# Filler matmuls in an attention kernel: one more use of TensorE wherever it has had little to do

## The chip, the cores and the metric

One core of one Trainium2 chip. The metric is the device time of one execution in microseconds (us), the median over several; lower is better. A run's profile gives a span that is about 1.7 us shorter than its device time (1177.7 against 1179.46 us for the profile of the kernel before).

## The reference, cut to what matters

Two attention blocks over 2048 tokens, width 1024, 32 heads of 32, in bf16; their outputs stand side by side.

```python
# A: full attention
qkv = (x @ wqkv) ...;  p = softmax(q k^T * 32**-0.5);  o = p v;  out_A = o @ wo
# B: four segments of 512 tokens, causal inside a segment, with a memory M, z carried between them
p = softmax(q k^T * 32**-0.5 + mask);  a_dot = p v
a_mem = (phi(q) M) / (phi(q) z + 1e-6)          # phi(t) = t+1 if t>0 else exp(t)
o = g * a_mem + (1 - g) * a_dot;  M += phi(k)^T v;  z += sum phi(k);  out_B = o @ wo
out = concatenate([out_A, out_B], -1)
```

In both blocks every score needs one exponential, which ScalarE computes. TensorE computes the projections, the scores and the sums (probabilities times V, and probabilities times ones for the denominators).

## The kernel before

The program is written by a planner that runs on the host. It keeps a clock for each engine with an estimated cost for every operation, and at each step it gives TensorE one of three things: scores (as soon as ScalarE has freed their banks), sums, or a piece of a "side" task such as a projection. If there is nothing to do, it lets TensorE's planned clock run on by 0.05 us and looks again. Each engine is then given its list in this order, with semaphores wherever the planner found a dependency. Planned times decide the order only.

```python
def op(self, eng, fn, r=(), w=(), cost=0.1, mode="F"):
    if eng == "PE":
        if mode != self.mode:
            cost += DRAIN                      # the planner's cost (0.105) of a change between scores, sums and full matmuls
        self.mode = mode
    op = Op(eng, self.n[eng], fn); ...
    t = self.free[eng]
    for d in op.deps:
        t = max(t, d.end + LAT)
    op.end = t + cost
    self.free[eng] = op.end
# ... (cut)
# the end of the planner's loop, reached when nothing could be given to TensorE
            if now < WARM and gap >= 0.15:     # WARM = 60: only in the first 60 us
                spare = [...]                  # a free bank
                if spare:
                    R.op("PE", lambda e, bank=spare[0]: e.matmul(self.ps[:, bank, :], self.ones[:, :], ...128x512 of ones...,
                                                                 start=True, stop=True), r=["ones"], w=[("ps", spare[0])], cost=MM)
                    gap = 0.0
                    continue
            R.free["PE"] = now + 0.05
            gap += 0.05
```

So fillers existed already, but only in the first 60 planned microseconds. A projection is a sum of eight matmuls into one bank and may be cut into parts, between which other work runs. The sums of the attention gather in one bank (`OLB`) over the 16 key tiles of a unit. A bank in which such a sum is under way must not be overwritten. (A second program for inputs that would overflow the exponential stands in the file too; it did not run here.)

Of the kernel before, what the change touches and what calls it, by code (L numbers as in the profile page):

```python
# [11 lines left out]
P = 128  # L12
# [9 lines left out]
MM = 0.213  # L22
# [14 lines left out]
class Recorder:  # L37
# [5 lines left out]
    def __init__(self, nc, es, tag):  # L43
        self.nc = nc
        self.tag = tag
        self.all = []
        self.n = {e: 0 for e in self.ENG}
        self.free = {e: 0.0 for e in self.ENG}
        self.last = {e: None for e in self.ENG}
        self.lastw, self.readers = {}, {}  # L50
        self.sem = {e: es.enter_context(nc.semaphore(f"{tag}_{e.lower()}")) for e in self.ENG if e != "SP"}
        self.ch_sem = [es.enter_context(nc.semaphore(f"{tag}_dma{i}")) for i in range(self.NCH)]
        self.ch_last = [None] * self.NCH
        self.ch_n = [0] * self.NCH
        self.ch_next = 0
        self.mode = None
        self.pipe = 0.0

    def _deps(self, eng, r, w):
        deps = []  # L60
# [18 lines left out]
            self.readers[k] = {}  # L79

    def op(self, eng, fn, r=(), w=(), cost=0.1, mode="F"):
        if eng == "PE":
            if mode != self.mode:
                cost += DRAIN
            self.mode = mode
        op = Op(eng, self.n[eng], fn)
        self.n[eng] += 1
        op.deps = self._deps(eng, r, w)
        self._note(op, r, w)
        t = self.free[eng]  # L90
        for d in op.deps:
            t = max(t, d.end + LAT)
        op.end = t + cost
        self.free[eng] = op.end
        self.all.append(op)
        self.last[eng] = op
        return op

    def dma(self, fn, r=(), w=(), issue=0.1, mb=0.25, q="SP", turn=False):
        c = self.ch_next  # L100
        self.ch_next = (c + 1) % self.NCH
        op = Op(f"D{c}", self.ch_n[c], fn)
        self.ch_n[c] += 1
        op.deps = self._deps(op.eng, r, w)
        if self.ch_last[c] is not None:
            op.deps.append(self.ch_last[c])
        self.ch_last[c] = op
        op.dma, op.queue = c, q
        self._note(op, r, w)
        t = self.free[q]  # L110
        for d in op.deps:
            t = max(t, d.end + LAT)
        self.free[q] = t + issue
        if turn:

            op.end = t + issue + 2.2
        else:
            self.pipe = max(self.pipe, t + issue) + mb / 0.22
            op.end = self.pipe + 1.5
        self.all.append(op)  # L120
        return op

    def resolve(self):
        names = list(self.ENG) + [f"D{i}" for i in range(self.NCH)]
# [109 lines left out]
SLOPE = 0.65  # L234
STICK = True
WARM = 60
TILES = (0, 1, 2, 3)
ON_ACT = ()
AHEAD = (6, 7)
# [8 lines left out]
class Kernel:  # L248
# [215 lines left out]
    def constants(self):  # L464
        R = self.R

        def pool(f, w, r=()):
            R.op("POOL", f, r=r, w=w, cost=0.3)
        R.op("DVE", lambda e: e.memset(self.PT[:, RING - 1, :], 1.0), w=[("PT", RING - 1)], cost=0.2)
        nb = sum(len(b) for b in SLOTS)  # L470
        for b in range(nb):
            R.op("DVE", lambda e, b=b: e.memset(self.ps[:, b, :], 0.0), w=[("ps", b)], cost=0.4)

        R.op("ACT", lambda e: e.activation(self.gcol[:, 0, :], self.PT[:, RING - 1, 0:8], ACTF.Exp), r=[("PT", RING - 1)], w=["gcol"], cost=1.5)
        pool(lambda e: e.memset(self.blk32[:, :], 1.0), ["blk32"])
        pool(lambda e: e.affine_select(self.blk32[:, :], self.blk32[:, :], pattern=[[-32, 4], [0, 8]],
                                       compare_op=ALU.is_ge, fill=0.0, base=0, channel_multiplier=1), ["blk32"])
        pool(lambda e: e.affine_select(self.blk32[:, :], self.blk32[:, :], pattern=[[32, 4], [0, 8]],
                                       compare_op=ALU.is_ge, fill=0.0, base=31, channel_multiplier=-1), ["blk32"])
        pool(lambda e: e.memset(self.ones[:, :], 1.0), ["ones"])  # L480
        pool(lambda e: e.memset(self.ident[:, :], 0.0), ["ident"])
        pool(lambda e: e.affine_select(self.ident[:, :], self.ident[:, :], pattern=[[-1, P]],
                                       compare_op=ALU.not_equal, fill=1.0, base=0, channel_multiplier=1), ["ident"])
        for i in range(2):
            pool(lambda e, i=i: e.memset(self.VB[i][:, :, :], 1.0), [("VB", i)])
        pool(lambda e: e.memset(self.maskbd[:, :], 1.0), ["maskbd"])
        pool(lambda e: e.affine_select(self.maskbd[:, :], self.maskbd[:, :], pattern=[[-32, 4], [0, 32]],
                                       compare_op=ALU.is_ge, fill=0.0, base=0, channel_multiplier=1), ["maskbd"])
        pool(lambda e: e.affine_select(self.maskbd[:, :], self.maskbd[:, :], pattern=[[32, 4], [0, 32]],
                                       compare_op=ALU.is_ge, fill=0.0, base=31, channel_multiplier=-1), ["maskbd"])  # L490
        pool(lambda e: e.memset(self.Mf[:, :, :], 0.0), [("Mf", g) for g in range(NG)])
# [226 lines left out]
    def mm_run(self, mms, r, w, each, k0=1):  # L718

        R = self.R  # L720
        i = 0
        while i < len(mms):
            room = yield ("pe", self.ready(r(i, i + k0)))
            k = max(k0, min(len(mms) - i, int((room - DRAIN) / each)))
            if len(mms) - i - k < k0:
                k = len(mms) - i
            part = mms[i:i + k]

            def f(e, part=part):
                for o, l, rh, a, z in part:  # L730
                    ins = e.matmul(o, l, rh, start=a, stop=z)  # L731
                return ins
            R.op("PE", f, r=r(i, i + k), w=w, cost=each * k)
            i += k

    def proj_T(self, W, wkey, xsl, xkeys, dst, dkeys, n=512):

# [297 lines left out]
        self.events.add(("out" + kind, c))  # L1035


    def spawn(self, gen, prio, name):
        t = Task(gen, prio if isinstance(prio, tuple) else (prio, 0), name)
        if t.req is not None:  # L1040
            self.tasks.append(t)
            self.tasks.sort(key=lambda t: t.prio)
# [69 lines left out]
    def schedule(self):  # L1112
# [2 lines left out]
        self.qA = [Item([Unit("A", NQ * g + c, g, c, 0, g % 2)]) for g in range(NG) for c in range(NQ)]  # L1115
        self.qB = [Item([Unit("B", 8 * s + g, g, s, half, g % 2) for half in (1, 0)]) for s in range(4) for g in range(NG)]
        self.pvq, self.nseq, self.ol_end, self.run = [], 0, 0.0, None
        self.tasks = []
        self.posA, self.ring, self.ring_busy, self.out_free = 0, 0, set(), [0, 1]
        self.slot_end = {s: 0.0 for s in SLOTS}  # L1120
        self.ring_len = LONG
# [11 lines left out]
        while True:  # L1133
# [52 lines left out]
            for what in (first, "side" if first == "pv" else "pv"):  # L1186
                if done:
                    break
                if what == "pv" and self.pvq:
                    u, st, part = self.pvq[0]  # L1190
                    c = DRAIN + 2 * u.steps[st][part][2] * 0.000417
                    t = u.steps[st][part][0]
                    v = ("vA", u.g, t // 4) if u.kind == "A" else ("vB", u.kn)
                    vk = ("VA", u.buf, t // 4) if u.kind == "A" else ("VB", u.buf)
                    if v in ev and self.ready([vk]) <= now and all((st, h) in u.pend for h in range(4)) \
                            and max(u.pend[(st, h)] for h in range(4)) + 0.15 <= now \
                            and (st > 0 or part > 0 or self.ol_end <= now) \
                            and (st < len(u.steps) - 1 or u.seq < 2 or ("fin", u.seq - 2) in ev) \
                            and (c <= room or len(self.ring_busy) > self.ring_len - 4):
                        if OLB not in self.bank_busy:  # L1200
                            self.emit_pv(u, st, part)
                            self.pvq.pop(0)
                            done = True
                elif what == "side":
                    if full and self.pvq and self.slots:

                        u, st, _ = self.pvq[0]
                        vt = self.ready([("VA", u.buf, u.steps[st][0][0] // 4)]) if u.kind == "A" else 0.0
                        if now < vt < now + 1.5:
                            room = min(room, max(0.5, vt - now))  # L1210
                    for t in self.tasks:
                        if t.req[0] == "pe" and self.satisfied(t.req, now) and room > 0.3:
                            self.resume(t, room)
                            done = True
                            break
# [4 lines left out]
                continue  # L1220
            if cur is None and not self.qA and not self.qB and not self.pvq and not self.tasks:
                break
            if now < WARM and gap >= 0.15:

                spare = [b for b in self.banks if b not in self.bank_busy and self.bank_end[b] <= now]
# [59 lines left out]
```

## Time and profile before

| | before |
|---|---|
| median of 4 runs | 1178.74 us (1176.4 to 1178.82) |
| ScalarE (ACT) busy | 1123.4 us, 95% |
| TensorE (PE) busy | 1069.7 us, 91% |
| mean granted TensorE clock | 0.972 |
| stretches at half clock between 60 and 1150 us | 8, together 54.6 us |

From the page of the kernel before: the busy times of the engines, the row of the granted clock (40 equal slices of the span, in tenths of full speed), the shares of the chain that ended last, and the largest group of instructions.

```profile
span 1177.7 us, 37192 instructions
PE 1069.7 (91%) x16874; PEld 480.1 (41%) x16874; DVE 795.6 (68%) x1368; ACT 1123.4 (95%) x1254; POOL 114.3 (10%) x192
...
PEclk9999999999999998989999998989999998999998
...
ACT 49%; PE 43%; DVE 6%; issue 1%; DMA 1%; DVEq 0%
...
L584 ACT ACTIVATE PT<-ps 128x1024 bf16<-128x1024 f32 (+1 forms) x1184 | 1074.0, 1043 | 31.7 <-PE ps L544 30.1
```

ScalarE is the engine to feed: 1184 exponentials, and most of its idle time (30.1 us) ended when scores arrived from TensorE. The clock row has five slices below 9 ahead of the tail, all in the middle. A slice is 29 us, so the row shows that the clock was cut but not how.

The table of windows shows how. The columns are the window, its length, then busy time and number of instructions of each engine, the granted clock, and the DMA share and rate. Kernel before:

```profile
core 0: us, PE busy (x) PEld busy (x) DVE busy (x) ACT busy (x) POOL busy (x), PEclk, DMA share, GB/s
447.35:450.77 3.42, 1.39 (x40) 0.69 (x40) 3.32 (x4) 3.42 (x6) 1.41 (x3) 1.00 0.00 0
450.77:461.01 10.24, 8.66 (x111) 3.48 (x104) 7.94 (x13) 9.04 (x11) 3.83 (x6) 0.50 0.01 2
519.03:522.45 3.42, 1.53 (x44) 0.57 (x32) 3.02 (x5) 3.42 (x5) 0.27 (x1) 1.00 0.00 0
522.45:532.69 10.24, 8.31 (x106) 3.38 (x103) 7.90 (x14) 9.30 (x11) 3.48 (x6) 0.50 0.01 2
```

In the 3.42 us before a stretch, TensorE is 41% or 45% busy while ScalarE is fully busy: TensorE waits for ScalarE (its longest pauses there are 1.27 and 1.23 us), and no other work stands in its list there. Then the clock goes to one half for 10.24 us, and now ScalarE is idle for 1.2 and 0.9 us of it: scores that came in time at full clock come too late.

### The profile page before, as it was taken

To read this page: it belongs to the slowest core of one execution; us is meant where nothing else is said; L and a number is where in the kernel's file an instruction comes from. 1 tells how busy PE (TensorE), PEld (TensorE's weight loads), DVE (VectorE), ACT (ScalarE), POOL (GpSimd) and SP (SyncE) were. 2 spreads that over 40 slices of the span, in tenths; PEclk is the share of its full clock that TensorE was granted. 3 is DMA by queue.
4 is the path that set the end of the run, shared out by engine and by line. 5 is a ranking of instruction groups with operands and counts; after the bars stand their busy time and mean duration, and the time that the engine had idled before them with its cause. 6 is when DMAs were issued, how large, how long until landed. Compare 5 with 4: busy or idle time off the path is not lost.

```text
span 1177.7 us, 37192 instructions
## 1 busy us (share of the span) xinstructions
PE 1069.7 (91%) x16874; PEld 480.1 (41%) x16874; DVE 795.6 (68%) x1368; ACT 1123.4 (95%) x1254; POOL 114.3 (10%) x192
## 2 busy tenths in 40 slices
PE   7999999999999987989999988889998998799995
PEld 3444444443444433434344433334443443344442
DVE  3366667678686787677768768777677786864444
ACT  5999999999999999999999998989999999999993
POOL 1010012011111011011110111111012011200000
PEclk9999999999999998989999998989999998999998
DMA  7544143152121230401311221111230121200111
GB/s 170 108 90 102 38 100 60 34 108 65 42 46 34 60 73 11 91 20 32 88 30 41 55 60 38 38 33 33 47 80 27 33 47 35 81 19 29 38 38 66
DMA packets 207050, 65.93 MB, mean 56 GB/s; under 512 B 200227, under 2 KB 200227, under 8 KB 206883
## 3 DMA queue, kind: packets, MB, share of 16 engines
q1 hardware_dynamic: 204512, 62.41, 23.6%
q8 instruction: 134, 2.20, 0.8%
q10 hardware_dynamic: 2370, 1.05, 0.4%
q14 instruction: 34, 0.27, 0.1%
HBM read 36.70 MB, written 8.39 MB: 38 GB/s over the span
## 4 chain that ended last, share of the span: by engine, by line
ACT 49%; PE 43%; DVE 6%; issue 1%; DMA 1%; DVEq 0%
ACT PT L584 47%; PE ps L731 23%; PE ps L633 11%; PE ps L544 8%; DVE SQ L656 2%; DVE OL L643 1%; ACT E L921 1%; DVE OL L691 0%; ACT WoB L584 0%; DMA OTA<-in_A_x_dram 0%; DVE outsb L1025 0%; DVE KQB L741 0%; DVE OL L682 0%; DVE KA L741 0%; DVE OTA L660 0%
## 5 line engine op out<-in xcount | busy, mean ns | idle before, releaser
L584 ACT ACTIVATE PT<-ps 128x1024 bf16<-128x1024 f32 (+1 forms) x1184 | 1074.0, 1043 | 31.7 <-PE ps L544 30.1
L633 PE MATMUL ps<-PT,ones 128*32 128x256 bf16 (+1 forms) x4736 | 285.7, 274 | 0.0
L633 PE MATMUL ps<-PT,VA 128*32 128x256 bf16 x3968 | 244.4, 278 | 17.5 <-ACT PT L584 9.9
L656 DVE RECIPROCAL SQ<-OL 128x128 f32<-128x128 f32 x256 | 242.4, 948 | 4.4
L544 PE MATMUL ps<-QA,KA 32*128 32x256 bf16 x4096 | 207.1, 277 | 35.0 <-ACT PT L584 26.5
L731 PE MATMUL ps<-xA,WA 128*128 128x512 bf16 (+1 forms) x792 | 200.7, 387 | 4.0 <-DVE amem L955 1.0
L731 PE MATMUL ps<-xB,WB 128*128 128x512 bf16 x768 | 195.0, 382 | 7.2 <-DVE den L941 3.6
L604 POOL TENSOR_SCALAR_AFFINE_SELECT PT<-PT 128x512 bf16<-128x512 bf16 x128 | 84.1, 659 | 788.5 <-ACT PT L584 783.0
L633 PEld LDWEIGHTS ps<-PT,VA 128*32 128x32 bf16 x3968 | 105.4, 96 | 108.0 <-issue 65.1
L544 PEld LDWEIGHTS ps<-QA,KA 32*128 32x128 bf16 x4096 | 61.3, 93 | 214.3 <-ACT PT L584 186.2
L633 PEld LDWEIGHTS ps<-PT,ones 128*32 128x32 bf16 x4736 | 128.0, 98 | 2.5
L643 DVE COPY OL<-ps 128x512 f32<-128x512 f32 x128 | 85.5, 668 | 32.5 <-PE ps L633 30.9
L731 PEld LDWEIGHTS ps<-xA,WA 128*128 128x128 bf16 x792 | 66.8, 100 | 94.8 <-issue 33.4
L731 PEld LDWEIGHTS ps<-xB,WB 128*128 128x128 bf16 x768 | 62.1, 97 | 94.0 <-issue 41.9
L948 DVE RECIPROCAL den<-den 128x128 f32<-128x128 f32 x96 | 91.0, 948 | 2.0
L1028 DVE CAST outsb<-ps 128x512 bf16<-128x512 f32 x56 | 38.3, 683 | 73.6 <-PE ps L731 71.4
L741 DVE CAST KQB<-ps 128x512 bf16<-128x512 f32 x64 | 43.6, 681 | 52.5 <-PE ps L731 52.4
L731 PE MATMUL ps<-WoB,OTB 128*128 128x512 bf16 x256 | 64.6, 382 | 2.0 <-DVE OTB L684 0.8
L731 PE MATMUL ps<-xA,OTA 128*128 128x512 bf16 x256 | 65.8, 388 | 0.1
L691 DVE SCALAR_TENSOR_TENSOR OL<-OL,SQ 128x256 f32<-128x256 f32 x128 | 58.9, 460 | 4.4
L633 PE MATMUL ps<-PT,VB 128*32 128x256 bf16 (+1 forms) x768 | 48.6, 271 | 10.8 <-DVE OL L643 8.6
L741 DVE CAST VT<-ps 128x512 bf16<-128x512 f32 x32 | 21.9, 685 | 44.7 <-PE ps L731 44.7
(78 smaller groups left out, 540.5 us busy)
## 6 DMA issues: line engine op xcount, KB each, us to landing
WB<-in_B_wk_dram SPq DMA_DIRECT2D x32, 256.0 KB, 3.0
WB<-in_B_wq_dram SPq DMA_DIRECT2D x32, 256.0 KB, 3.0
WB<-in_B_wv_dram SPq DMA_DIRECT2D x32, 256.0 KB, 3.3
out_dram<-outsb SPq DMA_DIRECT2D x32, 256.0 KB, 2.1
WA<-in_A_wqkv_dram SPq DMA_DIRECT2D x22, 256.0 KB, 3.6
WoB<-in_B_wo_dram SPq DMA_DIRECT2D x8, 256.0 KB, 3.4
xA<-in_A_wo_dram SPq DMA_DIRECT2D x8, 256.0 KB, 3.7
OTA<-in_A_x_dram ACTq DMA_DIRECT2D x2, 256.0 KB, 5.0
```

The lines of the kernel that those rows point to most:

```text
L544: ins = e.matmul(o, l, r, start=True, stop=True)
L584: op = R.op("ACT", lambda e: e.activation(self.pt(s0, n)[:, :, 0:width], self.ps[:, banks[0]:banks[0] + n, 0:width], ACTF.Exp, bias=cb, sc ...
L604: mo = R.op("POOL", lambda e, ap=ap, pat=pat: e.affine_select(ap, ap, pattern=pat, compare_op=ALU.is_ge, fill=0.0, base=0, channel_multipl ...
L633: ins = e.matmul(o, l, r, start=start, stop=end, skip_group_check=True)
L643: R.op("DVE", lambda e: e.tensor_copy(self.OL[x][:, :], self.ps[:, OLB, :]), r=[("ps", OLB)], w=[("OL", x)], cost=0.66)
L656: R.op("DVE", lambda e, cs=cs: e.reciprocal(rec[:, cs], L[:, cs]), r=[ko], w=[k], cost=0.93)
L691: R.op("DVE", lambda e: e.scalar_tensor_tensor(L, L, 1.0, rec, ALU.mult, ALU.add, accum_out=self.rng[:, u.seq:u.seq + 1]), r=[k, ko], w=[k ...
L731: ins = e.matmul(o, l, rh, start=a, stop=z)
L741: op = self.R.op("DVE", lambda e: e.tensor_copy(dst, self.ps[:, bank, 0:n]), r=[("ps", bank)], w=dkeys, cost=0.12 + n * 0.00105)
L921: ex = R.op("ACT", lambda e: e.activation(self.E[:, k0:k1, :], KQ[:, k0:k1, :], ACTF.Exp), r=[("KQB", b, k) for k in range(k0, k1)], w=["E ...
L948: R.op("DVE", lambda e, cs=cs: e.reciprocal(self.den[:, cs], self.den[:, cs]), r=["den"], w=["den"], cost=0.9)
L1028: op = R.op("DVE", lambda e, ns=ns, bank=bank, ob=ob: e.tensor_copy(self.outsb[ob][:, ns], self.ps[:, bank, :]), r=[("ps", bank)], w=[("ou ...
```

## The change

Its intent: keep TensorE's recent activity above a floor, so that the clock is not cut. When the planner finds nothing to do after 60 us, 0.1 us has passed so, and the planned work of the last 3 us is below 66%, it adds one 128x512 matmul. If a sum is under way, the filler has zero weights and is added onto that sum, which it is not to alter. If no sum is open, it overwrites a free bank with ones times ones. (`diag[0]` is a tile that this program does not use otherwise; it is set to zero at the start.)

```diff
+        if eng == "PE":
+            self.spans.append((op.end - bare, op.end))     # bare: the cost without DRAIN
+    def worked(self, now, span):
+        total = 0.0
+        for a, z in reversed(self.spans):
+            if z <= now - span:
+                break
+            total += z - max(a, now - span)
+        return total / span
+KEEP = 0.66
+    def keep_up(self):
+        R = self.R
+        onto = [("ps", OLB)] * self.ol_open + list(self.sums)
+        if not onto:
+            now = R.free["PE"]
+            for b in self.banks:
+                if b not in self.bank_busy and self.bank_end[b] + 0.3 <= now:
+                    R.op("PE", lambda e, b=b: e.matmul(self.ps[:, b, :], self.ones[:, :], ...ones, 512 columns...,
+                                                       start=True, stop=True), r=["ones"], w=[("ps", b)], cost=MM)
+                    return True
+            return False
+        bank = onto[0][1]
+        R.op("PE", lambda e: e.matmul(self.ps[:, bank, :], self.diag[0][:, :], ...ones, 512 columns...,
+                                      start=False, stop=False, skip_group_check=True), r=["zeros", "ones"], w=onto[:1], cost=MM)
+        return True
             if cur is None and not self.qA and not self.qB and not self.pvq and not self.tasks:
                 break
+            if not self.shifted and now >= WARM and gap >= 0.1 and R.worked(now, 3.0) < KEEP and self.keep_up():
+                gap = 0.0
+                continue
# ... (cut: bookkeeping of ol_open and sums, the memset of diag[0])
```

More of the change, by code (lines that the diff above doesn't have):

```diff
@@ L57, in __init__ @@
         self.pipe = 0.0
+        self.spans = []
     def _deps(self, eng, r, w):
@@ L81, in op @@
     def op(self, eng, fn, r=(), w=(), cost=0.1, mode="F"):
+        bare = cost
         if eng == "PE":
@@ L485, in constants @@
             pool(lambda e, i=i: e.memset(self.VB[i][:, :, :], 1.0), [("VB", i)])
+        if not self.shifted:
+            pool(lambda e: e.memset(self.diag[0][:, :], 0.0), ["zeros"])
         pool(lambda e: e.memset(self.maskbd[:, :], 1.0), ["maskbd"])
@@ L734, in mm_run @@
             i += k
+            if i < len(mms):
+                self.sums.add(w[0])
+            else:
+                self.sums.discard(w[0])
     def proj_T(self, W, wkey, xsl, xkeys, dst, dkeys, n=512):
@@ L1035, in out_proj @@
         self.events.add(("out" + kind, c))
+    def keep_up(self):
[5 more added lines that the diff above has]
+                if b not in self.bank_busy and self.bank_end[b] + 0.3 <= now:
+                    R.op("PE", lambda e, b=b: e.matmul(self.ps[:, b, :], self.ones[:, :], self.ones[:, :].unsqueeze(1).to_broadcast([P, 4, P]),
+                                                       start=True, stop=True), r=["ones"], w=[("ps", b)], cost=MM)
+                    return True
+            return False
+        bank = onto[0][1]
+        R.op("PE", lambda e: e.matmul(self.ps[:, bank, :], self.diag[0][:, :], self.ones[:, :].unsqueeze(1).to_broadcast([P, 4, P]),
+                                           start=False, stop=False, skip_group_check=True), r=["zeros", "ones"], w=onto[:1], cost=MM)
+        return True
     def spawn(self, gen, prio, name):
@@ L1117, in schedule @@
         self.pvq, self.nseq, self.ol_end, self.run = [], 0, 0.0, None
-        self.tasks = []
+        self.tasks, self.ol_open, self.sums = [], False, set()
         self.posA, self.ring, self.ring_busy, self.out_free = 0, 0, set(), [0, 1]
@@ L1201, in schedule @@
                             self.emit_pv(u, st, part)
+                            self.ol_open = not (st == len(u.steps) - 1 and part == 1)
                             self.pvq.pop(0)
```

## The prediction

> **What bounds the kernel.** ScalarE. The page shows it 95% busy (1123.4 of 1177.7 us), 1184 exponentials (mean 1043 ns) being 1074.0 us of that; in order of time they start every 0.90 us. Their tightest start-to-start times, with those of ScalarE's other work, add up to about 1103 us. TensorE is 91% busy, the chain of waits is 49% ScalarE and 43% TensorE.
>
> **What the change aims at.** The mean granted clock is 0.972. The clock records show eight stretches at half clock before the tail, all between 450 and 1021 us: three of 10.24 us, two of 6.83, three of 3.41, together 54.6 us. The table of windows shows how each starts: in the 3.4 us before it TensorE was only 0.39 to 0.54 busy. Counting each matmul as its columns at full clock (a quarter for 32-row or 32-column tiles), the window on the records' grid before each held 22 to 34% of array work; the lowest windows without a following drop held 34 to 38%. So the threshold seems to be about one third; scores and sums alone make 0.38 on average. In the half-clock stretches TensorE turns 1.00 busy and ScalarE runs dry: 450.8 to 461.0 had 1.2 us of idle ScalarE, with more just behind. Including 3 us after each, ScalarE starts lie 17.3 us later than at the tightest pace (about 14 us show as idle ScalarE). The other 15 us of slippage between 440 and 1040 us are not from the clock.
>
> [...] all stretches are multiples of 3.41 us at 0.50. [...]
>
> **What the change adds.** A 512-column matmul (0.38 us, at a rate of one in 0.21) with zero weights, where the planner sees 0.1 us without work and under 66% in its last 3 us. By my count of array work, 26% of the time lies below 0.66, the missing work is 48 us, and TensorE's real idle time there is 55 us. Estimate: 150 fillers (80 to 250), 9 in 10 between 440 and 1040 us. Nothing is removed.
>
> **On the critical path.** With fillers the sparse windows should hold 50 to 60% of work, so nearly all eight stretches should go: about 15.5 us back, almost one for one. Against this, a filler under way delays scores by up to 0.2 to 0.3 us, and scores return only 0.1 to 0.2 us before ScalarE needs them; most fillers hit nothing, I take 3 us in all, and the shifted order of the schedule adds plus or minus 3.
>
> **Prediction:** 1166.5 us, range 1159 to 1175. Faster by over 2% (below 1155.1) 0.05, within 2% 0.93, slower 0.02.
>
> **What would show it.** Mean granted clock 0.990 or more (the tail's drop of about 10 us remains); no half-clock stretch, or one, between 60 and 1150 us; a new group of 128x512 matmuls with 80 to 250 members; idle ScalarE down from 54 to about 40 us; waits of the exponential for scores down from 30.1 to about 16 us; TensorE busy time up to 15 us higher.
>
> **What would make it wrong.** Zero-weight matmuls not counted as activity (the drops stay); the planner's clock drifting from the real one, so that fillers land where they block scores or miss the sparse windows.

1178.74 less 15.5, plus 3 for the cost, is 1166.2, close to the 1166.5. The delay of 0.2 to 0.3 us and the 3 us in all are estimates, from the 0.38 us of such a matmul and the 0.21 us from one to the next. For the "0.1 to 0.2 us before ScalarE needs them": in the trace of the kernel before, the last of a block of eight score matmuls ends 0.14 us (median; quartiles 0.05 and 0.27) before the next exponential starts.

## The result, and the profile after

| | before | after |
|---|---|---|
| median of 4 runs | 1178.74 us | 1168.03 us (1166.16 to 1168.64) |
| mean granted clock, profiled run | 0.972 | 0.993 |
| half-clock stretches, 60 to 1150 us | 8, 54.6 us | 2, 6.8 us |
| ScalarE idle | 54.3 us | 44.1 us |
| exponentials waiting for scores | 30.1 us | 19.4 us |
| TensorE busy | 1069.7 us | 1080.9 us |

The ratio is 0.9911, with a 95% interval of 0.9894 to 0.9928: clear of 1. Ratios here are the mean time of one kernel's fast runs over that of the other's of the same rounds, so not quite the ratio of the medians quoted.

The same lines of the page after the change, and the two groups of fillers from the table of groups:

```profile
span 1166.3 us, 37422 instructions
PE 1080.9 (93%) x16987; PEld 482.5 (41%) x16987; DVE 791.6 (68%) x1368; ACT 1122.2 (96%) x1254; POOL 112.7 (10%) x193
...
PEclk9999999999999999999999999999999999999998
...
PE 46%; ACT 44%; DVE 6%; DMA 2%; SPq 1%; issue 1%; DVEq 0%
...
L600 ACT ACTIVATE PT<-ps 128x1024 bf16<-128x1024 f32 (+1 forms) x1184 | 1072.8, 1048 | 21.3 <-PE ps L560 19.4
```

```profile
L1067 PE MATMUL ps<-ones 128*128 128x512 bf16 x73 | 20.6, 383 | 0.8 <-DVE outsb L1045 0.7
L1072 PE MATMUL ps<-ones,diag 128*128 128x512 bf16 x40 | 13.8, 386 | 0.0
```

There are 113 fillers: 73 onto free banks and only 40 with zero weights onto a sum. By their starts, 28 lie before 440 us, 71 between 440 and 1040, and 14 after 1150 us, where ScalarE has no work left (0.00 us busy from there to the end).

The two stretches at half clock that are left, in the table of windows of the kernel after (same columns as above):

```profile
367.13:370.54 3.41, 1.75 (x38) 0.79 (x35) 3.31 (x8) 3.41 (x5) 1.32 (x3) 1.00 0.00 0
370.54:373.95 3.41, 3.41 (x15) 0.72 (x13) 2.40 (x6) 2.35 (x3) 0.00 (x0) 0.50 0.00 0
783.55:786.97 3.42, 1.47 (x48) 1.04 (x52) 3.32 (x8) 2.13 (x3) 0.00 (x0) 1.00 0.00 0
786.97:790.38 3.41, 3.41 (x72) 1.99 (x64) 1.38 (x4) 3.33 (x4) 0.00 (x0) 0.50 0.02 5
```

They have the form of those before. Neither sparse window contains a filler. The timeline of the second says why (start, time, engine and line, then in brackets the idle time before it and what ended it):

```profile
782.66 0.40 PE L560 MATMUL ps<-QA,KA 32*128 32x256 bf16 x8
...
784.76 0.68 DVE L659 COPY OL<-ps 128x512 f32<-128x512 f32 x1
...
785.50 0.29 PE L649 MATMUL ps<-PT,VA 128*32 128x256 bf16 x4 [2.44 <-DVE OL L659]
```

Here TensorE stood for 2.44 us at a sum that waited for VectorE's copy. It started nothing else in that time, and the list has no filler at that point: only the planner's clock decides where fillers go.

**Where the time went.** Take for every ScalarE instruction of the steady work the shortest regular distance to the next one's start (903 ns for a 1024-column exponential), add them, and call the rest slippage. The slippage is split into what falls into a half-clock stretch or the 3 us after it, and what does not.

| us | before | after |
|---|---|---|
| until the first exponential | 12.1 | 10.0 |
| shortest distances, summed | 1093.3 | 1093.3 |
| slippage, first 60 us | 5.6 | 9.0 |
| slippage at half clock and 3 us after | 17.3 | 2.7 |
| other slippage after 60 us | 30.3 | 32.1 |
| from the last exponential's start to the end | 19.2 | 19.1 |
| span | 1177.7 | 1166.3 |

The clock gave back 14.6 us, and other slippage grew by 1.8 us. Up to 60 us the two traces differ by 1.3 us in all (the first and third rows together). That is not the change's doing: none of its fillers is planned there, and the repeated profile of the same kernel (e5 below) shows 5.6 us of slippage again. But it is in part the same effect. In this one trace TensorE stood for 2.16 us, until 19.53 us, for a DMA that brought input (0.98 us busy of the 3.40 us up to 19.0), the clock was at one half from 19.0 us on for 3.41 us, and ScalarE waited 3.36 us for the scores that came then. The trace does not part the DMA's share from the clock's.

### The profile page after: what moved, and what is told of

It reads as the page before. It is cut to its first block, busy times and chain, and to the rows that moved or that the text cites. A ratio compares the mean times of both kernels' runs of the same rounds, so it can differ in the third digit from the quotient of the medians.

```text
span 1166.3 us, 37422 instructions
## 1 busy us (share of the span) xinstructions
PE 1080.9 (93%) x16987; PEld 482.5 (41%) x16987; DVE 791.6 (68%) x1368; ACT 1122.2 (96%) x1254; POOL 112.7 (10%) x193
## 4 chain that ended last, share of the span: by engine, by line
PE 46%; ACT 44%; DVE 6%; DMA 2%; SPq 1%; issue 1%; DVEq 0%
ACT PT L600 42%; PE ps L747 25%; PE ps L649 12%; PE ps L560 8%; DVE SQ L672 2%; DVE OL L659 1%; ACT E L941 1%; SPq L410 1%; DMA xA<-in_A_x_dram 1%; ACT WoB L600 0%; DMA out_dram<-outsb 0%; DVE OL L707 0%; DMA PKt<-PH 0%; DVE den L961 0%; DVE OTA L676 0%
## 5 line engine op out<-in xcount | busy, mean ns | idle before, releaser
L600 ACT ACTIVATE PT<-ps 128x1024 bf16<-128x1024 f32 (+1 forms) x1184 | 1072.8, 1048 | 21.3 <-PE ps L560 19.4
L649 PE MATMUL ps<-PT,ones 128*32 128x256 bf16 (+1 forms) x4736 | 281.0, 271 | 0.0
L560 PE MATMUL ps<-QA,KA 32*128 32x256 bf16 x4096 | 203.9, 273 | 29.6 <-ACT PT L600 20.5
L747 PE MATMUL ps<-xA,WA 128*128 128x512 bf16 (+1 forms) x792 | 195.7, 378 | 6.0 <-DMA xA<-in_A_x_dram 2.2
L649 PE MATMUL ps<-PT,VB 128*32 128x256 bf16 (+1 forms) x768 | 45.8, 260 | 8.6 <-DVE OL L659 7.3
```

The costliest lines, as they stand in the source:

```text
L560: ins = e.matmul(o, l, r, start=True, stop=True)
L600: op = R.op("ACT", lambda e: e.activation(self.pt(s0, n)[:, :, 0:width], self.ps[:, banks[0]:banks[0] + n, 0:width], ACTF.Exp, bias=cb, sc ...
L649: ins = e.matmul(o, l, r, start=start, stop=end, skip_group_check=True)
L747: ins = e.matmul(o, l, rh, start=a, stop=z)
```

## The experiments

The theory (C): the fillers hold TensorE's clock at full speed, and that is the whole gain. The rival (O): a filler takes time on the planner's clock, so the planner orders all other work differently, and the new order is by luck the better one. Further questions: do zero weights count as activity, do both kinds of filler matter, and what does a filler cost. Each of the three groups of four (e1 to e4, e5 to e8, e9 to e12) ran on one chip in 5 rounds with the kernel before; all outputs were correct. Clocks in the table are means over a kernel's runs.

| run | fillers | ratio to before | 95% interval | mean us | mean clock |
|---|---|---|---|---|---|
| before, beside e1 to e4 | none | | | 1179.0 | 0.970 |
| e1 tiny | 113, one column wide | 0.9993 | 0.9976 to 1.001 | 1178.5 | 0.969 |
| e2 old order | 112, order of before | 0.9900 | 0.9882 to 0.9919 | 1167.4 | 0.994 |
| e3 zero all | 113, all zero weights | 0.9917 | 0.9899 to 0.9935 | 1169.5 | 0.992 |
| e4 tiny sums | 73 on free banks | 0.9907 | 0.9888 to 0.9926 | 1168.4 | 0.989 |
| e5 the change again | 73 + 40 | 0.9908 | 0.9889 to 0.9927 | 1168.6 | 0.992 |
| e6 tiny free | 40 on sums | 0.9983 | 0.9964 to 1.0003 | 1176.5 | 0.975 |
| e7 double | 226 | 0.9923 | 0.9907 to 0.9940 | 1170.0 | 0.997 |
| e8 old order, more | 171, order of before | 0.9918 | 0.9901 to 0.9934 | 1168.7 | 0.994 |
| e9 old order, few | 54, order of before | 0.9903 | 0.9882 to 0.9925 | 1167.1 | 0.991 |
| e10 share 0.80 | 136, new order | 0.9902 | 0.9879 to 0.9925 | 1166.5 | 0.992 |
| e11 free bank first, 0.80 | 136, order of e10 | 0.9912 | 0.9886 to 0.9939 | 1168.2 | 0.991 |
| e12 share 0.80, tiny | 136, one column wide | 0.9961 | 0.9939 to 0.9983 | 1174.0 | 0.973 |

### e1: the new order without the fillers' work

```diff
-  e.matmul(self.ps[:, b, :], self.ones[:, :], ...512 columns..., start=True, stop=True)
+  e.matmul(self.ps[:, b, 0:1], self.ones[:, :], self.ones[:, 0:1], start=True, stop=True)
-  e.matmul(self.ps[:, bank, :], self.diag[0][:, :], ...512 columns..., start=False, ...)
+  e.matmul(self.ps[:, bank, 0:1], self.diag[0][:, :], self.ones[:, 0:1], start=False, ...)
```

The planned costs stay, so the order of all instructions is that of the change. (Checked in the traces: the lists of the weight loads and of the other engines are the same.) The fillers and the granted clock of this run:

```profile
L1067 PE MATMUL ps<-ones 128*128 128x1 bf16 x73 | 6.2, 170 | 1.7 <-DVE outsb L1045 1.7
L1072 PE MATMUL ps<-ones,diag 128*128 128x1 bf16 x40 | 5.5, 173 | 0.3 <-issue 0.3
...
PEclk9999999999999978999999997999999999999998
```

> The changed kernel's order of work, every filler still there but one column wide instead of 512, so that it does next to no work in the array. Theory C (the gain is the clock that the fillers hold up): back to about 1178 us (1174 to 1182), mean granted clock about 0.97, several half-clock stretches between 400 and 1040 us. Rival O (the fillers only made the planner choose a luckier order): stays at about 1168 us although the clock drops to 0.97.

Measured: 1178.26 us median, ratio 0.9993, clock 0.969. The whole gain is gone although every instruction and its order are those of the change; only 511 of 512 columns of each filler are missing. So 113 instructions that stand in the trace with 170 and 173 ns each in the mean left the clock as it was without them (0.970). The profile shows 12 half-clock stretches (64.9 us) between 60 and 1150 us and 17.6 us of slippage at them, as before. Rival O falls.

### e2: the old order with fillers

```diff
     def keep_up(self):
+        free, mode = R.free["PE"], R.mode
+        try:
+            return self.filler()               # the body of keep_up
+        finally:
+            R.free["PE"], R.mode = free, mode  # the planner's clock does not see the filler
-            if ... gap >= 0.1 and R.worked(now, 3.0) < KEEP and self.keep_up():
-                gap = 0.0
-                continue
+            if ... gap >= 0.1 and now >= since + MM + 0.1 and R.worked(now, 3.0) < KEEP and self.keep_up():
+                since = now
```

Compared list by list, the order of all other work is that of before, plus the one memset and 112 fillers.

> The order of all other work exactly as in the kernel before; 112 full-width fillers put into it without the planner's clock knowing of them. Theory C: 1165 to 1171 us, clock 0.99 or more. Rival O: about 1178 us, whatever the clock does.

Measured: 1167.06 us median, ratio 0.9900, clock 0.994. The whole gain without any new order. Since the order is the same, the k-th ScalarE instruction of one trace can be set against the k-th of the other. Its lead over the kernel before, with the half-clock stretches of before that lie in between:

| time in before, us | lead of e2, us | between this row and the one above |
|---|---|---|
| 450.3 | 0.28 | |
| 464.5 | 2.76 | stretch at 450.8, 10.24 us long |
| 522.6 | 2.79 | none |
| 535.8 | 5.24 | stretch at 522.4, 10.24 us |
| 703.9 | 5.21 | none |
| 716.8 | 7.77 | stretch at 703.4, 10.24 us |
| 983.2 | 10.77 | three stretches, 13.7 us in all; e2 has one itself |
| 993.9 | 13.14 | stretch at 983.2, 6.83 us |
| 1040.7 | 14.05 | stretch at 1017.4, 3.41 us |

In the rows with no stretch between them the lead does not move, and it steps up at each stretch. Here are about the same pieces of work as in the windows of before, now in the table of windows of e2:

```profile
447.90:450.80 2.90, 2.59 (x44) 0.93 (x46) 2.80 (x5) 2.90 (x6) 1.72 (x3) 1.00 0.02 6
450.80:459.10 8.30, 7.21 (x133) 3.35 (x126) 8.12 (x14) 8.30 (x12) 3.52 (x6) 1.00 0.00 0
516.60:519.80 3.20, 2.82 (x39) 0.99 (x38) 3.13 (x5) 3.20 (x5) 0.41 (x1) 1.00 0.02 5
519.80:528.70 8.90, 6.39 (x122) 3.06 (x126) 8.04 (x15) 8.90 (x12) 3.34 (x6) 1.00 0.01 2
```

TensorE is 89% and 88% busy where it was 41% and 45%, the clock stays at 1.00, ScalarE has no idle time, and the ten ScalarE instructions that start in each stretch, up to the start of the next one, take 8.3 and 8.8 us where they took 10.6 and 11.3. Of the lead of 14.05 us, 11.9 are left in the span: 0.4 us is lost near 1093 us of the time in before, 1.1 us between 1130 and 1137, and the rest around the end. The timeline of e2 shows what the 1.1 us is:

```profile
1118.85 0.69 DVE L1048 CAST outsb<-ps 128x512 bf16<-128x512 f32 x1 [4.03 <-DMA out_dram<-outsb]
1119.60 1.04 PE L747 MATMUL ps<-xA,OTA 128*128 128x512 bf16 x4 [1.04 <-DVE outsb L1048]
1121.02 1.94 ACT L600 ACTIVATE PT<-ps 128x1024 bf16<-128x1024 f32 x2 [0.92 <-PE ps L560]
```

VectorE waited 4.03 us for the DMA of an output buffer that it wanted to fill again, TensorE for VectorE, and ScalarE 0.92 us for TensorE. In before, the one such DMA wait between 1050 and 1150 us is 2.1 us and ScalarE does not wait there. Why the DMA took longer was not tested.

### e3: only zero weights

```diff
-  e.matmul(self.ps[:, b, :], self.ones[:, :], ...), r=["ones"], w=[("ps", b)]
+  e.matmul(self.ps[:, b, :], self.diag[0][:, :], ...), r=["zeros", "ones"], w=[("ps", b)]
```

> The changed kernel with the 73 fillers on free banks given zero weights too, so that all 113 multiply by zero; same order. If zero weights count as activity like others: 1168 us within 2 us, clock about 0.993. If they do not count: the drops come back where the 73 stood, clock about 0.975, 1175 us or more.

Measured: 1169.54 us median, ratio 0.9917, clock 0.992, against 0.9908 and 0.992 for the change itself (e5, on another chip). Multiplying by zero holds the clock as well as multiplying by one.

### e4 and e6: one kind of filler at a time

e4 makes the 40 zero-weight fillers on sums one column wide, e6 the 73 on free banks; the edits are the two halves of e1's.

> The changed kernel with only the 40 zero-weight fillers (on sums under way) cut to one column; the 73 on free banks stay. Theory C with work counted alike wherever it goes: some of the drops come back, clock about 0.98 to 0.99, 1170 to 1174 us. If the fillers on free banks do all the work: 1168 us as the change. If those on sums do it all: 1177 us.

> The changed kernel's order, the 73 fillers on free banks cut to one column, the 40 zero-weight ones on sums kept. If each filler is worth the same: clock about 0.98, 1173 to 1176 us. If the ones on sums are worth little, as their removal suggested (1168.4 us mean without them): clock 0.975 or less and 1176 us or more.

Measured: e4 1168.95 us median (ratio 0.9907, clock 0.989), e6 1176.01 us (0.9983, 0.975). The 73 alone give the whole gain in time; the 40 alone about a fifth of it by the ratios, and by e6's interval anything from nothing to two fifths. The 40 do something for the clock: without them the profile has 6 stretches (23.9 us) instead of the 2 and 5 (6.8 and 17.1 us) of the change's two profiles. But no time comes of it within the error of these runs. By the table of slippage, e4 has 7.2 us at half clock and 30.9 us other; the change has 2.7 and 32.1 in one profile, 7.6 and 32.9 in the other. So these profiles show no net gain from the 40 zero-weight fillers; whether they cost what they spare at the clock is not shown. Nor is it shown why the 73 do so much more: zero weights are not the reason (e3), but the two kinds also stand at different times.

### e5: the change once more

> The change itself once more, for comparison on the same chip: ratio 0.991 within 0.002, clock 0.991 to 0.995.

Measured: 1168.72 us median, ratio 0.9908. Single runs ranged from 1165.47 us (clock 0.994) to 1172.05 us (0.990), and the profile shows five stretches where the first had two, at other places. So which sparse places are caught differs from run to run. One reason, by these two traces, is that the grid of 3.41 us on which the stretches begin lies elsewhere in each: they begin 1.90 us past a multiple of 3.413 us in the first profile and 0.81 us past it in e5's. Near 783 us, e5's own grid cuts the sparse place into windows of 0.375 and 0.402 of array work (counted as in "What cuts the clock", spread over the recorded times), and the clock stayed. The first profile's grid laid over e5's trace gives one window of 0.232 there, and the first profile fell there.

### e7 and e8: more fillers

e7 issues every filler twice, without telling the planner; e8 is e2 with the floor out of reach (`KEEP = 2.0`), so that every planned gap gets fillers.

> The changed kernel's order, every filler issued twice, the planner not told. The additional 113 matmuls take 24 us of TensorE at 0.213 us each. If fillers sit in idle time: clock 0.995 or more, 1166 to 1170 us. If each delays what follows it by its whole length: about 1190 us.

> The order of before with a filler in every gap that the planner sees (171 instead of 112). Theory: the last half-clock stretches go too, worth 1 to 2 us at most, against 59 more fillers that cost 0 to 2 us: 1165 to 1169 us, clock 0.995 or more.

Measured: e7 1170.59 us (ratio 0.9923, clock 0.997); e8 1168.24 us (0.9918, 0.994), its clock just under the 0.995 expected. The second 113 fillers of e7 lift the clock by 0.005 against e5, and the run is still 1.4 us longer by the means, which the overlapping intervals do not bear out. Other slippage is 36.4 us in e7's profile against 32.9 in e5's: 3.5 us for 113 matmuls, or some 30 ns each, far from the 216 ns from start to start of such a pair in e7's trace. With e8 against e2 the additional 59 bring nothing, and no cost shows: other slippage is the same within 0.3 us. Both differences also hold waits that are not the fillers', such as e2's 0.9 us for the DMA, so they are rough. Fillers are cheap; that they cost anything is not shown.

### e9: fewer

```diff
-KEEP = 0.66
+KEEP = 0.45        # in e2's kernel
```

> The order of before with 54 fillers (only where the planner sees under 45% of its last 3 us) instead of 112. If half the fillers in the emptiest places are enough: clock 0.99 or more and 1166 to 1169 us. If the planner's clock is too rough for that: clock 0.980 to 0.988, and by the 0.41 us per us of lost clock that e5 gives against before, 1170 to 1174 us.

Measured: 1167.01 us median, ratio 0.9903, clock 0.991: as good as twice the number. Half the fillers suffice.

### e10 to e12: towards a better version

e10 sets `KEEP = 0.80` in the change. The planner then finds an order that it holds for 4 us shorter. e11 tries a free bank first, e12 is e10 with one-column fillers.

> The change with its share raised from 0.66 to 0.80: 136 fillers (82 with zero weights on sums, 54 on free banks), and an order that the planner itself holds for 4 us shorter. Candidate for a better version: clock 0.993 to 0.996; 1164 to 1167 us if the planner's order is really better, 1168 to 1170 us if only the 23 more fillers show.

> The same order as e10 with 136 fillers, put onto a free bank wherever there is one (98) and onto a sum under way only else (38). If fillers on sums delay the sums: 1 to 2 us faster than e10. If it does not matter where a filler writes: the same as e10 within 1.5 us.

> The order of e10 with all fillers one column wide: what that order is worth by itself. If the order is neutral: 1177 to 1180 us at clock 0.97. If the order is 4 us better as the planner says: 1174 to 1176 us.

Measured: e10 1165.45 us (ratio 0.9902), e11 1167.68 us (0.9912), e12 1174.61 us (0.9961, clock 0.973). This new order alone is worth about 0.4%, so an order can matter by some 4 us; in the change it did not (e1). The two gains need not add: 0.9961 times the change's 0.9908 would be 0.987, e10 measured 0.9902, and the intervals leave both open. e10 has the lowest median of all and 1166.5 us by the mean, but its interval (0.9879 to 0.9925) covers the change's 0.9908. It beats the kernel before; that it beats the change is not shown. The expectation that a free bank is the better place (e11 faster by 1 to 2 us) was not met: e11 was 1.6 us slower by the means, with one run of 1173.43 us in it, and the intervals overlap, so where a filler writes stays undecided.

### What cuts the clock

In six traces with all matmuls recorded (before, after, e5 to e8; in the others some 10% of the 512-column matmuls of the projections are missing), the time from 50 us on, up to 20 us before the end, can be cut into 3.41 us windows on the grid of the clock's records. Count each matmul, in the window in which it starts, as its columns at full clock (a 512-column one as the planner's 0.213 us, where the traces of before and after have 216 ns from one to the next; a quarter of that where it uses 32 rows or columns, since four such sums of 256 columns start every 109 ns there) and ask what follows a window at full clock:

| array work in the window | windows | followed by half clock |
|---|---|---|
| up to 0.33 | 17 | 17 |
| 0.34 to 0.41 | 31 | 10 |
| above 0.41 | all others | none |

TensorE was still 28 to 63% busy in the windows that were followed by half clock. So TensorE need not stop for the clock to fall. That the middle class falls either way is mostly the way of counting: with each matmul spread evenly over its recorded time, all 26 windows with up to 0.360 were followed by half clock, one of the 4 between 0.361 and 0.373, and none of the 1858 above. This border was found afterwards on the same six traces, and a count by columns is only a stand-in: what the hardware goes by was not shown. Scores and sums alone make 0.33 between 60 and 1150 us of the kernel before. So where TensorE has nothing else to do it stands at about the border.

## Why the prediction was right

- **The time**: forecast 1166.5 us (1159 to 1175); measured 1168.03. The terms erred in both directions (below), so part of the closeness is luck.
- **The mechanism**, "about 15.5 us back, almost one for one": right. 14.6 us at half clock vanished in the profile (9.7 in e5's), e1 and e2 show that the fillers' work and not the new order made the gain, and the matched instructions of e2 gain it at the stretches.
- **The cost**, "I take 3 us in all": other slippage grew by 1.8 us in the profile of after and 2.6 in e5's; another 113 came with 3.5 us in e7, another 59 with none in e8.
- **"The shifted order of the schedule adds plus or minus 3"**: measured 0.9993 in e1 (0.9976 to 1.001), so between 2.8 us faster and 1.2 us slower.
- **"Nearly all eight stretches should go", "no half-clock stretch, or one"**: too good. Two are left in one profile and five in the other. In the first profile this is 0.9 us of the shortfall (14.6 in place of 15.5), the first 60 us are another 1.3, and 1.2 us less cost than forecast makes up for part. The forecast had named the reason, "the planner's clock drifting from the real one, so that fillers ... miss the sparse windows", and the 2.44 us wait at 783 us is such a place.
- **"150 fillers (80 to 250), 9 in 10 between 440 and 1040 us"**: 113, of which 71, or 63%, lie there. 14 are spent after 1150 us.
- **"A 512-column matmul ... with zero weights"**: incomplete. The diff has two branches, and 73 of the 113 go through the one with ones on a free bank. For the time it made no difference (e3), but it was these 73 that brought the gain.
- **Idle ScalarE "to about 40 us"** was 44.1, **waits for scores "to about 16 us"** 19.4; the left-over stretches and, in this profile, a slower start (3.4 us more slippage in the first 60 us, with a half-clock stretch of its own at 19.0 us) are in them. TensorE's busy time rose by 11.2 us, within the "up to 15".
- **"all stretches are multiples of 3.41 us at 0.50"**: so they are before the tail, in the profiles of before (3.41, 6.83 and 10.24 us) and after (3.41 us). The border, **"about one third"**, was near the measured one, about 0.34 to 0.41 of array work (0.36 with the matmuls spread); "scores and sums alone make 0.38 on average" counts to 0.33.

That a zero-weight matmul may be laid onto an open sum rests here on the outputs alone: all were correct, with 40 such fillers in the change (e5).

## What to carry to other kernels

An engine that is not the busiest can still set part of the time through its clock, as TensorE (91% busy, ScalarE 95%) did here: 17.3 us of slippage with 54.6 us at half clock, 2.7 with the 6.8 us that the fillers left. Look for half-clock stretches in fine windows, and for the sparse window ahead of each, before asking what the engine "waits" for. Fillers in idle time can cost little (some 30 ns each or nothing here, against 216 ns from one to the next), and a floor of 0.45 was as good as 0.66; they must stand in the instruction list at the place where the engine really idles, which a host-side clock hits only mostly (neither sparse window that still fell in the profile of after held one). To tell such an effect from a lucky reordering, run both crossings: the new order with fillers made tiny, and the old order with full fillers.
